# A decode step with attention over a long cache: 210 small transfers of zeros behind every second load

## The chip, the cores and the metric

One core of one Trainium2 chip runs the whole program. The time is that of one launch on the device in microseconds (us). Two runs of the kernel before are shown, 698.48 and 698.58 us, with the median 698.53. A third launch was taken with the hardware profiler; its own time was 698.42 us.

## The reference

One token of each of two sequences goes through attention over a cache of 4096 positions and 32 heads, and then through a small dense block; both are modulated by a condition `c`. Cut to what matters:

```python
mod = (silu(c) @ w_mod).reshape(2, 6, 1, -1)         # w_mod 512 x 3072
sa, ca, ga, sb, cb, gb = (mod[:, i] for i in range(6))
h = layernorm(x) * (1 + ca) + sa                     # x: 2 x 1 x 512
q = (h @ wq).reshape(2, 1, 32, 128).transpose(0, 2, 1, 3)
p = softmax(einsum("bhqd,bhkd->bhqk", q, k_cache) * 128 ** -0.5)
o = einsum("bhqk,bhkd->bhqd", p, v_cache)            # caches: 2 x 32 x 4096 x 128
x = x + ga * (o.transpose(0, 2, 1, 3).reshape(2, 1, 4096) @ wo)
h = layernorm(x) * (1 + cb) + sb
x = x + gb * (mish(h @ w1 + b1) @ w2)                # w1 512 x 1376
```

Everything is float32. The two caches are by far the most of it: 268 of the 297 MB that the launch reads.

## The kernel before

Each weight and each head of the caches is used once, so the kernel streams them all through on-chip memory. `stream` (on the host) packs the pieces into 36 loads. Nearly all of them are one transfer of 128 partitions by 16,384 floats, 64 KB a partition and 8.4 MB in all: the keys of one head (`BIG`, 8192 floats a partition) and other pieces, mostly half heads of the values (`HALF`), that fill it up. The last ones are cut smaller.

`load(n)` takes a buffer called `room` from a pool of three and issues the load's transfers on SP's queue (L141). `used(*keys)` is called when a piece has had its last reader; it issues load n+3 when every piece of load n is used. So SP's queue holds an issue, a wait for a buffer, an issue, and so on, in the order of the loads. Instructions go to each engine in the order in which the program writes them; the framework puts in the waits. It gives each transfer on SP's queue one of eight semaphores in turn (the lanes), and at the end of the program it waits for all of them.

For each of the 32 heads, VectorE multiplies the keys by the query (`products`, L318) and sums over 128 elements (`sums`, L321), each once over 128 x 8192 floats; `row_max` and `soft_max` follow with small instructions. TensorE multiplies the values with the softmax's numerators (`weighted_v`, L359) and does the small projections, ScalarE the exponentials. Load n+1 and n+2 are in flight while head n is worked on.

Behind the last head come the output projection, the second layer norm, the dense block, and the last lines: the result `y`, a buffer of the pool `work` under the tag `sq`, is made by two VectorE instructions (L564, L565) and 32 of its rows of 512 B are stored (L566). GpSimd clears some constants at the start, `cx` first (L160), and SP closes the program at L636.

Of the kernel before, what the change touches and what calls it, by code (L numbers as in the profile page):

```python
# [8 lines left out]
F32 = mybir.dt.float32  # L9
# [4 lines left out]
P = 128  # L14
# [11 lines left out]
OUT_STEP = 4  # L26
AHEAD = (14, 22)
ROW = 2 * BIG


def stream():
# [13 lines left out]
    def size(x):  # L45
        return sum(SIZES[key[0]] for key in x)

    loads = [[([("m01", 0), ("wq", 0), ("wq", 1)], (4 * W,)), ([("k", 0)], (BIG,))]]
    for _ in range(1, HEADS):
        row = []  # L50
        while size(row) < ROW:
            room = ROW - size(row)
            row += order.pop(next(i for i, x in enumerate(order) if size(x) <= room))
        loads.append([(row, (ROW,))])
    last = [("v", h, i) for h in range(HEADS - 4, HEADS) for i in range(2)]
# [14 lines left out]
def kernel(  # L70
# [3 lines left out]
    head: bass.AP,  # L74
    b1c: bass.AP,
    out: bass.AP,
):


# [6 lines left out]
    nc = tc.nc  # L86
# [16 lines left out]
    work = ctx.enter_context(tc.tile_pool(name="work", bufs=2))  # L103
# [12 lines left out]
    def take(t, keys):  # L116
        lo = 0
        for key in keys:
            kind, n = key[:2]
            part = t[:, lo : lo + SIZES[kind]]  # L120
            lo += SIZES[kind]
            if kind == "k":
                k_t[n] = part.rearrange("p (j d) -> p j d", d=DH)
            elif kind == "v":
                v_t[n, key[2]] = part.rearrange("p (c n) -> p c n", n=512)
            elif kind in ("wq", "wo"):
                (wq_t if kind == "wq" else wo_t)[n] = part.rearrange("p (k n) -> p k n", k=G)
            else:
                w_t[kind] = part.rearrange("p (k n) -> p k n", k=NCH if kind == "w2" else G)
# [4 lines left out]
    def load(n):  # L134

        t = kvp.tile([P, ROW], F32, tag="room", name=f"room{n}", bufs=3)
        lo = 0
        for keys, srcs in loads[n]:
            take(t[:, lo:], keys)
            for src in srcs:  # L140
                nc.sync.dma_start(out=t[:, lo : lo + src.shape[-1]], in_=src)  # L141
                lo += src.shape[-1]

    loaded = 0

    def used(*keys):

        nonlocal loaded
        done.update(keys)
        while loaded < len(loads) and (  # L150
            loaded < 3 or all(key in done for keys, _ in loads[loaded - 3] for key in keys)
        ):
            load(loaded)
            loaded += 1
# [16 lines left out]
        out=fold, in_=ident.rearrange("p (g r) -> p r g", g=G), axis=AX.X, op=ALU.add  # L171
# [3 lines left out]
        out=mean_w, in0=fold[:, None, :].to_broadcast([P, G, R]), scalar1=1.0 / D, scalar2=None, op0=ALU.mult  # L175
# [4 lines left out]
        out=half, in_=ident.rearrange("p (b r) -> p r b", b=B), axis=AX.X, op=ALU.add  # L180
# [373 lines left out]
    for n in range(NCH):  # L554
        for t in range(G):
# [4 lines left out]
                start=(n == 0),  # L560
                stop=(n == NCH - 1),
            )
    y = work.tile([P, P], F32, tag="sq", name="y", bufs=1)
    nc.vector.tensor_tensor(out=y, in0=yps[:, :P], in1=mod[5], op=ALU.mult)  # L564
    nc.vector.tensor_tensor(out=y, in0=y, in1=x2, op=ALU.add)  # L565
    nc.sync.dma_start(out=out, in_=y[::OUT_STEP, :])  # L566


def _lay_out(np, a):
# [70 lines left out]
```

## Time and profile before

| | |
|---|---|
| median of two runs | 698.53 us |
| the profiled execution's own time | 698.42 us |
| its span, from first to last instruction | 696.6 us |
| VectorE busy | 587.7 us (84%) |
| TensorE matmuls busy | 283.8 us (41%) |
| ScalarE, GpSimd busy | 44.0 us, 4.2 us |
| read from DRAM | 297.22 MB, 427 GB/s over the span |
| written to DRAM | 0.02 MB |

The DMA part of a profile counts packets. One row of a transfer, contiguous on both sides, is one packet, and the packets of a transfer are dealt over the core's 16 DMA engines. A share of "16 engines" is packet time divided by sixteen times the length of the stretch looked at; a packet is counted whole where it starts, so a short stretch can show over 100%. q1 is SP's queue, q10 ScalarE's, q8 and q14 bring instructions. "SPq" rows are SP's instructions: issuing a transfer, or waiting (EVENT_SEMAPHORE); their durations are minimum, median and maximum in ns.

### The profile page before, as it was taken

How to read it: one execution, taken by the hardware profiler on the slowest of the kernel's cores; microseconds unless marked ns; L12 is line 12 of the kernel's file. 1: busy time of each engine (PE TensorE's matmuls, PEld its weight loads, DVE VectorE, ACT ScalarE, POOL GpSimd, SP SyncE). 2: the span in 40 equal slices, each digit the busy share in tenths (PEclk: the TensorE clock that was granted, in tenths of full speed). 3: DMA queues.
4: the chain of work that ended last, by engine and by line, in shares of the span. 5: the costliest groups of instructions: out<-in, count | busy, mean ns of one | idle time of the engine just before them, and what ended most of it. 6: DMA issues, size and time to landing. Idle time of an engine off the chain costs nothing.

```text
span 696.6 us, 3912 instructions
## 1 busy us (share of the span) xinstructions
PE 283.8 (41%) x1636; PEld 102.4 (15%) x1636; DVE 587.7 (84%) x220; ACT 44.0 (6%) x168; POOL 4.2 (1%) x19
## 2 busy tenths in 40 slices
PE   3403334335245615335232806234333526224686
PEld 1200001001011201102100301011101101001234
DVE  3799899999999999999999999999999999899002
ACT  1000000000000000000000000000000000000010
POOL 2000000000000000000000000000000000000000
PEclk9855666667566665656585756666575657555789
DMA  9999999999999999999999999999999999999996
GB/s 392 452 421 421 426 474 421 419 429 421 467 422 425 429 425 456 429 425 426 433 448 429 426 429 437 440 430 429 433 437 437 429 425 422 452 427 420 423 422 270
DMA packets 6706, 297.49 MB, mean 427 GB/s; under 512 B 888, under 2 KB 928, under 8 KB 1184
## 3 DMA queue, kind: packets, MB, share of 16 engines
q1 hardware_dynamic: 6528, 297.23, 98.9%
q8 instruction: 13, 0.21, 0.1%
q10 hardware_dynamic: 160, 0.01, 0.0%
q14 instruction: 5, 0.04, 0.0%
HBM read 297.22 MB, written 0.02 MB: 427 GB/s over the span
## 4 chain that ended last, share of the span: by engine, by line
DMA 69%; DVE 28%; PE 2%; issue 0%; SPq 0%; ACT 0%; DVEq 0%
DMA room<-in_load 69%; DVE room L318 14%; DVE s L321 14%; PE ov L359 1%; PE qps L291 1%; PE modps L247 1%; PE yps L556 0%; SPq L141 0%; DVE m L334 0%; DVE hcw L280 0%; ACT q L292 0%; PE hps L237 0%; DVE y L564 0%; DVE hq L270 0%; DVE hq L271 0%
## 5 line engine op out<-in xcount | busy, mean ns | idle before, releaser
L318 DVE TENSOR_TENSOR room<-room,q 128x8192 f32<-128x8192 f32 x32 | 278.2, 8692 | 46.8 <-DMA room<-in_load 42.4
L321 DVE TENSOR_REDUCE s<-room 128x64 f32<-128x8192 f32 x32 | 277.9, 8683 | 0.4 <-DVE m L334 0.3
L359 PE MATMUL ov<-room,e 128*32 128x512 f32 x1024 | 176.4, 842 | 80.1 <-ACT e L337 63.9
L330 PE MATMUL mt<-d,same 128*128 128x64 f32 x64 | 18.2, 378 | 195.8 <-DVE d L328 195.8
L359 PEld LDWEIGHTS ov<-room,e 128*32 128x32 f32 x1024 | 39.2, 145 | 188.6 <-issue 133.8
L337 ACT ACTIVATE e<-s,m 64x64 f32<-64x64 f32 x64 | 22.1, 345 | 556.6 <-DVE m L334 555.8
L330 PEld LDWEIGHTS mt<-d,same 128*128 128x128 f32 x64 | 13.1, 254 | 225.8 <-DVE d L328 179.3
L291 PE MATMUL qps<-room,hcw 128*128 128x512 f32 x64 | 43.4, 844 | 4.8 <-DMA room<-in_load 4.0
L345 PE MATMUL l<-l,ones 128*128 128x8 f32 x16 | 4.6, 358 | 75.1 <-ACT e L337 75.1
L382 PE MATMUL otp<-pick,o 128*128 128x8 f32 (+2 forms) x72 | 13.4, 313 | 33.9 <-ACT o L374 32.0
L291 PEld LDWEIGHTS qps<-room,hcw 128*128 128x128 f32 x64 | 16.8, 274 | 26.4 <-issue 20.5
L374 DVE COPY o<-ov 128x256 f32<-128x256 f32 x1 | 0.4, 425 | 22.6 <-ACT o L374 22.6
L382 PEld LDWEIGHTS otp<-pick,o 128*128 128x128 f32 x72 | 12.6, 263 | 42.3 <-ACT o L374 39.4
L345 PEld LDWEIGHTS l<-l,ones 128*128 128x128 f32 x16 | 3.8, 296 | 76.5 <-ACT e L337 76.5
L334 DVE TENSOR_REDUCE m<-mt 128x1 f32<-128x64 f32 x32 | 6.9, 217 | 7.6 <-PE mt L330 7.6
L390 PE MATMUL att<-room,ot 128*32 128x512 f32 x62 | 10.1, 709 | 5.2 <-DMA room<-in_load 4.7
L337 ACT ACTIVATION_READ_ACCUMULATOR e<-s,m 64x1 f32 x64 | 11.8, 185 | 0.0
L328 DVE TENSOR_SCALAR d<-half,m 128x64 f32<-128x64 f32 x32 | 8.1, 254 | 1.1
L247 PE MATMUL modps<-room,ct 128*32 128x128 f32 (+1 forms) x160 | 8.1, 346 | 2.3 <-DMA room<-in_load 2.2
L326 DVE TENSOR_REDUCE m<-s 128x1 f32<-128x64 f32 x32 | 7.0, 217 | 0.9
L374 ACT COPY o<-ov 128x512 f32<-128x512 f32 (+1 forms) x9 | 5.0, 561 | 25.9 <-PE ov L359 25.7
L247 PEld LDWEIGHTS modps<-room,ct 128*32 128x32 f32 x160 | 5.0, 121 | 4.6 <-issue 4.4
(101 smaller groups left out, 60.6 us busy)
## 6 DMA issues: line engine op xcount, KB each, us to landing
room<-in_load SPq DMA_DIRECT2D x4, 4096.0 KB, 25.0
room<-in_load SPq DMA_DIRECT2D x1, 7168.0 KB, 39.1
room<-in_load SPq DMA_DIRECT2D x1, 3072.0 KB, 26.2
room<-in_load SPq DMA_DIRECT2D x3, 1024.0 KB, 28.3
room<-in_load SPq DMA_DIRECT2D x1, 2400.0 KB
room<-in_load SPq DMA_DIRECT2D x1, 2304.0 KB, 20.4
room<-in_load SPq DMA_DIRECT2D x1, 1376.0 KB, 15.8
room<-in_load SPq DMA_DIRECT2D x2, 256.0 KB, 22.8
```

Of the source, the lines that this page charges most:

```text
L247: nc.tensor.matmul(ps[R * g : R * (g + 1)], lhsT=ct[:, k, :], rhs=t[:, k, :].rearrange("p (m n) -> p m n", m=n)[:, :, P * g : P * (g + 1)] ...
L291: nc.tensor.matmul(ps, lhsT=hcw[:, k, :], rhs=wq_t[ch][:, k, :], start=(k == 0), stop=(k == G - 1))
L318: nc.vector.tensor_tensor(out=k_t[h], in0=k_t[h], in1=qv, op=ALU.mult)
L321: nc.vector.tensor_reduce(out=s_t[h], in_=k_t[h], axis=AX.X, op=ALU.add)
L326: nc.vector.tensor_reduce(out=m_t[h][:, 0:1], in_=s_t[h], axis=AX.X, op=ALU.max)
L328: nc.vector.tensor_scalar(out=d, in0=half, scalar1=m_t[h][:, 0:1], scalar2=None, op0=ALU.mult)
L330: nc.tensor.matmul(mps[h], lhsT=same, rhs=d, start=True, stop=True)
L337: nc.scalar.activation(e_t[i][own_b, :, M * i + 4 * b : M * i + 4 * b + 4], s_t[h][own_b].rearrange("p (c m) -> p c m", m=4), AF.Exp, bias ...
L345: nc.tensor.matmul(lps[n], lhsT=ones, rhs=sum_t[n % 2], start=True, stop=True)
L359: nc.tensor.matmul(ov[bank][R * g : R * (g + 1), :], lhsT=e_t[h % HC][:, NB // 2 * part + c, :], rhs=v_t[h, part][:, c, :], start=(first a ...
L382: nc.tensor.matmul(tps[:, x], lhsT=o_t[m], rhs=pick_t[n][:, m, x], start=(m == 0), stop=(m == 3),)
L390: nc.tensor.matmul(att[R * i : R * (i + 1), :], lhsT=ot_t[n % 2][:, i, :], rhs=wo_t[n][:, i, :], start=(n == 0), stop=(n == H // HC - (2 i ...
```

## The change

Behind each odd load from 3 to 29, `load` issues 15 transfers more on SP's queue: the n-th takes n rows of 96 floats (384 B) from `mark`, a buffer of zeros, to its own place in a new DRAM output `marks` that nobody reads. These 210 transfers and the store of the result count on a semaphore of their own, `out_done`, and are taken out of the framework's lanes (`no_tile_sem_insts`). At the end of the program, behind the framework's own closing waits, SP waits until the semaphore stands at 16 x 211 and clears it. `mark` is cleared by GpSimd ahead of its other constants, and `mark` and `y` are buffers of their own instead of pool buffers. No instruction on TensorE, VectorE or ScalarE is added or moved, and the loads keep their order, lanes and waits; the store no longer waits for a lane.

```diff
+MARKED = range(3, 31, 2)
...
             for src in srcs:
                 nc.sync.dma_start(out=t[:, lo : lo + src.shape[-1]], in_=src)
                 lo += src.shape[-1]
+        if n in MARKED:
+            for rows in range(1, 16):
+                m = nc.sync.dma_start(out=marks[MARKED.index(n), rows, :rows], in_=mark[:rows]).then_inc(out_done, 16)
+                tc.no_tile_sem_insts.add(m.ins.name)
 
     loaded = 0
+    nc.gpsimd.memset(mark, 0.0)
...
-    y = work.tile([P, P], F32, tag="sq", name="y", bufs=1)
     nc.vector.tensor_tensor(out=y, in0=yps[:, :P], in1=mod[5], op=ALU.mult)
     nc.vector.tensor_tensor(out=y, in0=y, in1=x2, op=ALU.add)
-    nc.sync.dma_start(out=out, in_=y[::OUT_STEP, :])
+    store = nc.sync.dma_start(out=out, in_=y[::OUT_STEP, :]).then_inc(out_done, 16)
+    tc.no_tile_sem_insts.add(store.ins.name)
...
+    args["out_done"] = nc.alloc_semaphore("out_done")
+    args["mark"] = nc.alloc_sbuf_tensor("mark", [16, 96], F32).ap()
+    args["marks"] = nc.dram_tensor("marks", (len(MARKED), 16, 16, 96), F32, kind="ExternalOutput").ap()
+    args["y"] = nc.alloc_sbuf_tensor("y", [P, P], F32).ap()
     with tile.TileContext(nc) as tc:
         tile_adaln_decode_kernel(tc, **args)
+    nc.sync.wait_ge(args["out_done"], 16 * (1 + 15 * len(MARKED)))
+    nc.sync.sem_clear(args["out_done"])
```

The marked line of the issue is L150 in the changed kernel.

More of the change, by code (lines that the diff above doesn't have):

```diff
@@ L76 @@
     out: bass.AP,
+    out_done,
+    y,
+    mark,
+    marks,
 ):
```

## The prediction

> **What bounds the kernel now.** I read the page first: the span, the slices, the DMA part, the shares of the chain, the two costliest groups.
>
> ```profile
> span 696.6 us, 3912 instructions
> ...
> PE 283.8 (41%) x1636; PEld 102.4 (15%) x1636; DVE 587.7 (84%) x220; ACT 44.0 (6%) x168; POOL 4.2 (1%) x19
> ...
> DMA  9999999999999999999999999999999999999996
> ...
> DMA packets 6706, 297.49 MB, mean 427 GB/s; under 512 B 888, under 2 KB 928, under 8 KB 1184
> ## 3 DMA queue, kind: packets, MB, share of 16 engines
> q1 hardware_dynamic: 6528, 297.23, 98.9%
> ...
> q10 hardware_dynamic: 160, 0.01, 0.0%
> ...
> DMA 69%; DVE 28%; PE 2%; issue 0%; SPq 0%; ACT 0%; DVEq 0%
> ...
> L318 DVE TENSOR_TENSOR room<-room,q 128x8192 f32<-128x8192 f32 x32 | 278.2, 8692 | 46.8 <-DMA room<-in_load 42.4
> L321 DVE TENSOR_REDUCE s<-room 128x64 f32<-128x8192 f32 x32 | 277.9, 8683 | 0.4 <-DVE m L334 0.3
> ```
>
> The 16 DMA engines are busy for 98.9% of their time with SP's queue (q1). VectorE is busy too (84% of the span), but it waits for loads: of its 46.8 us idle ahead of L318, 42.4 end with a load. The chain in order of time shows the rhythm:
>
> ```profile
> 256.49 8.69 DVE room L318
> 265.18 0.14 DVE m L334
> 265.32 8.60 DVE s L321
> 273.97 40.52 DMA room<-in_load
> 314.52 8.69 DVE room L318
> ```
>
> From one L318 to the next on this chain are 314.52 - 256.49 = 58.03 us. There are three buffers, so load n+3 is issued when head n has been summed; the step is three loads, 19.34 us each. VectorE's pair takes 8.69 + 8.69 = 17.4 us of it, so about 2 us lie free. The 40.5 us of DMA are a load that stands behind an earlier one on the engines. A DMA engine that gets more work is therefore late at once, with no cover from VectorE. How full an engine is, a DMA view of 100 to 600 us says:
>
> ```profile
> DMA packets 3708, 216.16 MB, mean 432 GB/s; under 512 B 401, under 2 KB 401, under 8 KB 401
> ...
> q1 hardware_dynamic: 3697, 216.01, 99.9%
> q8 instruction: 8, 0.13, 0.1%
> ```
>
> A full load is 128 packets of 64 KB, eight to an engine, plus one small packet an engine: 401 is 25 loads by 16 and one. On the page, 888 packets under 512 B are the 128 rows of the bias load and 760 = 47 x 16 + 8 others, which fits one semaphore packet for each engine of 45 loads, the bias and the store, and eight for the eight-row load of `cx`. (q10: 128 + 16 + 8 + 8 = 160.) So a transfer of eight rows used eight engines. One 64 KB packet lasts 0.999 x 16 x 500 us / 3296 = 2.42 us, and 0.1% of 8000 us, 8 us with a rounding of 4 either way, is left over at 400 load ends: 10 to 30 ns for each, semaphore packet and next load following.
>
> **The added transfers on the engines.** MARKED has 14 loads (3, 5, ... 29), with 15 transfers of 1 to 15 rows behind each. If a transfer of n rows uses n engines and always begins at the same one, that engine carries 15 row packets and 15 semaphore packets a group, 14 x 15 = 210 pairs in all, and the last engine almost none; if the beginning moves round, each has 14 x 120 / 16 = 105 pairs. No row shows which engines are used. I take 210, the dearer end; 105 stays as the lower bound.
>
> The nearest thing to such a pair is the output store: 32 rows of 512 B, two to an engine, on idle engines. The DMA view from 695.25 to 695.46 us, then from 695.44 to 695.46 us (one semaphore packet), then its issue and landing:
>
> ```profile
> DMA packets 48, 0.02 MB, mean 78 GB/s; under 512 B 16, under 2 KB 48, under 8 KB 48
> ...
> q1 hardware_dynamic: 48, 0.02, 30.3%
> ```
>
> ```profile
> q1 hardware_dynamic: 1, 0.00, 2.8%
> ```
>
> ```profile
> out<-y SPq DMA_DIRECT2D x1, 16.0 KB, 1.7
> ...
> 694.06 0.55 SPq L566 DMA_DIRECT2D out<-y  x1
> ```
>
> The semaphore packet is 0.028 x 16 x 20 ns = 9 ns. All 48 are 0.303 x 16 x 210 = 1018 ns; less 16 x 9, a row of 512 B is 27 ns. A row of 384 B lies on the line between 4 B at 9 and 512 B at 27: 23 ns. A pair is 32 ns of packets; with the idle 10 to 30 ns at a load's end it is 42 to 62. I take 42, the low end, as rows of a store followed each other in the 210 ns window: 210 x 42 = 8.8 us, between 6.7 (no gap) and 13.0 (30 ns).
>
> From that goes the slack of the loaded engine. Engines do not run level: of load 31's semaphore packets, seven stand in 602.40 to 603.40 us, eight in 604.20 to 605.10, the last in 605.60 to 605.80:
>
> ```profile
> DMA packets 15, 0.52 MB, mean 524 GB/s; under 512 B 7, under 2 KB 7, under 8 KB 7
> ```
>
> ```profile
> DMA packets 19, 0.72 MB, mean 801 GB/s; under 512 B 8, under 2 KB 8, under 8 KB 8
> ```
>
> ```profile
> DMA packets 2, 0.07 MB, mean 328 GB/s; under 512 B 1, under 2 KB 1, under 8 KB 1
> ```
>
> An engine is ahead of the last one by 0 to 3.3 us, in the mean by (7 x 2.8 + 8 x 1.05) / 16 = 1.75 us. A load is complete with its slowest engine, so 8.8 - 1.75 = 7.0 us arrive at the end; behind load 29 nothing is marked, and the last loads only pass the delay on.
>
> The Trainium skill ("DMA: Bandwidth & Descriptors", Why a DMA increments its semaphore by 16 and not by 1) says that a transfer on SP's queue takes the lowest-numbered k engines, k the largest number up to 16 that divides the slowest dimensions of both sides. By it the 15-row transfer uses 15 engines and the same engine is hit each time: my 210, and the count of eight for `cx` agrees; with a moving start the sum would be 698.4 + 105 x 42 ns = 702.8 us.
>
> **The issues on SP.** SP's rows of the load line:
>
> ```profile
> L141 SPq DMA_DIRECT2D room<-in_load x45: 327/328/530, 0.7 to 670.0; - x45
> L141 SPq EVENT_SEMAPHORE  x36: 17/17522/17887, 12.9 to 662.0; - x36
> ...
> DMA to landing us min/median/max: 12.2/40.5/59.2
> ```
>
> Fifteen issues at 0.33 us, or at the store's 0.55, are 4.9 to 8.2 us. Behind them waits only the next load's issue, and SP sits 17.5 us (median) in its wait for that load's buffer: hidden, with 9 us left. Were that cover gone, the next load would still have about 19 us of queued work ahead of it on the engines. Some 210 more instructions are fetched too: q8 brought 0.13 MB / 8 = 16 KB at a time, 0.6 us of one engine at 64 KB in 2.42; a fetch or two more, mostly on other engines, is counted at nothing.
>
> **Start and end.** The clear of `mark` stands ahead of that of `cx` on GpSimd, and the first mark waits for it.
>
> ```profile
> 0.00:13.00 13.00, 1.71 (x6) 1.51 (x7) 5.13 (x19) 1.93 (x4) 3.79 (x18) 1.00 0.89 364
> ...
> SPq L636 <- DMA out<-y: 0.9, 1, 0.9
> ```
>
> GpSimd's 18 clears take 3.8 us of the first 13 (the fifth busy column), while the first load takes 12.2 to land (the least of the landings above); one more costs nothing, and the first group comes only behind load 3. At the end SP waited 0.9 us for the store at L636; that wait now stands behind the framework's closing steps, with a clear of the semaphore after it. Between 1 us gained and 1 lost, I take 0. The own buffer for `y` adds no wait.
>
> **Sum.** The profiled execution's own time is 698.42 us (span 696.6 and 1.8 around it), 0.1 below the median of 698.53. 698.4 + 7.0 = 705.4; I say 705.
>
> **Rivals.** (1) Slower: a pair holds its engine until the write has landed, so pairs cannot overlap. The store's last packet ends near 695.46 and its landing is at 694.06 + 1.7 = 695.76: 0.3 us of landing a pair at least, 1.7 at most. 210 x 0.3 - 1.75 = +61, 760 us; at 1.7 us +355, 1054. It decides from 210 pairs of 76 ns, where 2% is passed. Against it speak the 10 to 30 ns at a load's end; for it, that a load has one semaphore packet per engine in 19 us, whose stall a buffer may hide, and a group has 15 in a row. Chance 0.12.
>
> The Trainium skill (same page, Anatomy of one DMA, written for GpSimd's path) calls most of a small transfer's fixed 2 us a wait for the write's receipt, ahead of the semaphore. Our store's 1.7 us agrees in size; whether the engine stands idle meanwhile no run here shows.
>
> (2) A row of 384 B costs double, as a read and a write: 2 x 27 + 9 + 10 = 73 ns a pair, 210 x 73 = 15.3, less 1.75: 712 us; up to 722 if it is threefold and gaps are 30 ns (210 x 120). Nothing in the trace is a store under 512 B. Chance 0.13, half of it over 2%.
>
> The Trainium skill (same page, Specifications) says that under 512 B the engine does a read-modify-write; no run here shows its price.
>
> (3) Two loads and 15 marks are 17 transfers in flight on one queue; if it holds fewer, SP is stopped in mid-group until the marked load drains, and engines run dry.
>
> ```profile
> 667.40 2.98 SPq L141 DMA_DIRECT2D room<-in_load  x6
> ```
>
> Six issues in 2.98 us went through unhindered, and no issue of 45 took over 0.53; 17 at once are not seen. With some six marks left (6 x 0.35), the next load's issue and its 1.2 us to the first packet (695.25 - 694.06), 3.6 us of dry engines a group: 14 x 3.6 = 50, 748 us. Chance 0.10.
>
> (4) It does less than it says: pairs spread over all engines (702.8), or the loaded engine has the full 3.3 us of slack and pairs cost 25 ns (+2, 700.4). Chance 0.10.
>
> **How the numbers follow.** The forecast, 700 to 712, has 0.54; the rivals 0.12, 0.13, 0.10 and 0.10; 0.01 stays for a gain over 2%, which 16 full engines exclude but for a reason I don't see. 2% (14 us) is about what a measurement here tells from no change. Within it: 0.54 + 0.10 + 0.07 = 0.71; slower 0.06 + 0.12 + 0.10 = 0.28. The range 699 to 725 takes in the forecast, (4) and (2), and leaves (1) and (3) out.
>
> **What would show it.** Right: q1 has 14 x 240 = 3360 packets more; in a marked load's end the engines' semaphore packets spread by 0.6 us a group, one engine falling behind the rest until it ends each load; the L318 step grows from 58.0 to about 59 us. Wrong: a step longer by several us with idle gaps on one engine (1) or on all (3), an L150 issue of many us on SP (3), or marked groups that move no engine against another (4).

## The result and the profile after

The changed kernel takes 721.51 us (721.29 and 721.74), the kernel before 698.53: a ratio of 1.0327, 95% interval 1.0311 to 1.0344, 23.0 us more where 6.5 were forecast. The profiled execution took 721.74 us. Its page, with the span, the packets, SP's DMA queue, the chain's shares and VectorE's two large groups:

```profile
span 720.0 us, 4123 instructions
...
DMA packets 10067, 298.15 MB, mean 414 GB/s; under 512 B 4248, under 2 KB 4288, under 8 KB 4544
...
q1 hardware_dynamic: 9888, 297.88, 97.7%
...
DMA 70%; DVE 27%; PE 2%; issue 0%; SPq 0%; ACT 0%; DVEq 0%
...
L328 DVE TENSOR_TENSOR room<-room,q 128x8192 f32<-128x8192 f32 x32 | 278.1, 8692 | 71.1 <-DMA room<-in_load 65.2
L331 DVE TENSOR_REDUCE s<-room 128x64 f32<-128x8192 f32 x32 | 277.9, 8683 | 0.4 <-DVE m L344 0.3
```

q1 has 9888 - 6528 = 3360 packets more, as forecast. VectorE's work is the same to 0.1 us; its idle time ahead of L328 (L318 before) grew by 24.3 us, 22.8 of them waits for loads. So the time came in through late loads. The chain in order of time (start, length, what) shows by how much for each group:

```profile
142.74 8.69 DVE room L328
151.53 8.70 DVE s L331
160.29 42.45 DMA room<-in_load
202.76 8.69 DVE room L328
211.55 8.70 DVE s L331
220.30 44.36 DMA room<-in_load
264.76 8.69 DVE room L328
```

Steps of 60.02 and 62.00 us alternate, as one marked load or two fall into three. Six loads with three groups take 122.0 us, against 2 x 58.03 before: 2.0 us a group, three times the 0.6 that the forecast's working gives (15 x 42 ns). 14 x 2.0 less the spread of 3.3 us that the engines had from before would be 24.7.

Where are the 2.0 us? Two DMA views of one engine's group: the 16 semaphore packets and 15 rows in 202.25 to 202.63 us, then the one 64 KB packet that starts behind them. The third is a 64 KB packet of the kernel before, in a stretch of the same length (10 ns, so the share is its length over 160 ns).

```profile
DMA packets 31, 0.01 MB, mean 15 GB/s; under 512 B 31, under 2 KB 31, under 8 KB 31
...
q1 hardware_dynamic: 31, 0.01, 7.8%
```

```profile
q1 hardware_dynamic: 1, 0.07, 2542.5%
```

```profile
q1 hardware_dynamic: 1, 0.07, 1511.9%
```

The small packets are as quick as forecast: 31 of them in 0.38 us, 25 ns a pair. But the packet behind them lasts 25.425 x 160 = 4.07 us, where 15.119 x 160 = 2.42 is usual. 0.38 + 1.65 = 2.03 us: the group's whole price, and most of it is paid by the next load. So something behind the packets' records backs up, by inference; the experiments ask what.

SP's rows, the marks' and the loads':

```profile
L150 SPq DMA_DIRECT2D marks<-mark x210: 251/296/410, 42.7 to 572.1; - x105
```

```profile
L146 SPq EVENT_SEMAPHORE  x36: 17/15722/19452, 13.0 to 686.6; - x36
```

No issue is held up (0.41 us at most), and SP still waits 15.7 us (median) ahead of a load. At the end, from the store's issue at 718.24 us to the span's end are 1.76 us; before, 694.06 to 696.6, 2.54:

```profile
718.24 0.55 SPq L575 DMA_DIRECT2D out<-y  x1
```

### The profile page after: what moved, and what is told of

It is laid out like the page before. It is cut to its first block, busy times and chain, and to the rows that moved or that the text cites. A ratio compares the mean times of both kernels' runs of the same rounds, so it can differ in the third digit from the quotient of the medians.

```text
span 720.0 us, 4123 instructions
## 1 busy us (share of the span) xinstructions
PE 286.4 (40%) x1636; PEld 105.6 (15%) x1636; DVE 587.6 (82%) x220; ACT 44.0 (6%) x168; POOL 4.3 (1%) x20
## 3 DMA queue, kind: packets, MB, share of 16 engines
q1 hardware_dynamic: 9888, 297.88, 97.7%
## 4 chain that ended last, share of the span: by engine, by line
DMA 70%; DVE 27%; PE 2%; issue 0%; SPq 0%; ACT 0%; DVEq 0%
DMA room<-in_load 70%; DVE room L328 13%; DVE s L331 13%; PE ov L369 1%; PE qps L301 1%; PE modps L257 1%; SPq L146 0%; PE yps L566 0%; DVE m L344 0%; DVE hcw L290 0%; PE hps L247 0%; ACT q L302 0%; DVE y L573 0%; DVE hq L281 0%; DVE hq L280 0%
## 5 line engine op out<-in xcount | busy, mean ns | idle before, releaser
L328 DVE TENSOR_TENSOR room<-room,q 128x8192 f32<-128x8192 f32 x32 | 278.1, 8692 | 71.1 <-DMA room<-in_load 65.2
L302 ACT ACTIVATE q<-qps 128x512 f32<-128x512 f32 x8 | 4.8, 598 | 14.6 <-PE qps L301 14.5
```

Of the source, the lines that this page charges most:

```text
L328: nc.vector.tensor_tensor(out=k_t[h], in0=k_t[h], in1=qv, op=ALU.mult)
```

## The experiments

Three theories stood for the long packet. Landing: each transfer's semaphore packet holds its engine's write side until what it stands for has landed, and what is read behind it backs up. Short rows: writing a row of 384 B is dear. Late reads: small packets fill the engine's look-ahead, so that the next 64 KB are read late. Medians are beside a kernel before of 698.55 to 698.59 us; what is written to `marks` is read by nobody. The count that the last wait expects and the shape of `marks` follow each edit; such lines are not shown (`...`).

**Rows of 512 B**, taken from `ones` (made a buffer of its own, as in the other kernels that read it).

```diff
-                m = nc.sync.dma_start(out=marks[MARKED.index(n), rows, :rows], in_=mark[:rows]).then_inc(out_done, 16)
+                m = nc.sync.dma_start(out=marks[MARKED.index(n), rows, :rows], in_=ones[:rows]).then_inc(out_done, 16)
...
-    args["marks"] = nc.dram_tensor("marks", (len(MARKED), 16, 16, 96), F32, kind="ExternalOutput").ap()
+    args["marks"] = nc.dram_tensor("marks", (len(MARKED), 16, 16, 128), F32, kind="ExternalOutput").ap()
```

> The same 210 transfers, with rows of 512 B in place of 384 B. In the changed kernel the 64 KB packet behind 15 pairs (row and semaphore) on one engine took 4.06 us in place of 2.42. Short rows (writing a row under 512 B is what holds the engine): that packet is back at 2.4 us and the time at 702 to 705 us. Landing (each transfer's semaphore packet holds the engine's write side until its row has landed) and late reads (the small packets take the place of the look-ahead, so that the next 64 KB are read late): the packet stays near 4.06 us and the time at 721 to 722 us.

721.67 us, 1.0329 (1.0299 to 1.0359). A 64 KB packet behind a group, in a stretch of 10 ns:

```profile
q1 hardware_dynamic: 1, 0.07, 2477.5%
```

24.775 x 160 = 3.96 us. Short rows are out.

**One transfer with 15 rows for each engine**, so 15 rows and one semaphore packet.

```diff
-            for rows in range(1, 16):
-                m = nc.sync.dma_start(out=marks[MARKED.index(n), rows, :rows], in_=mark[:rows]).then_inc(out_done, 16)
-                tc.no_tile_sem_insts.add(m.ins.name)
+            m = nc.sync.dma_start(
+                out=marks[MARKED.index(n), :, :, :96], in_=ones[:16, None, :96].to_broadcast([16, 15, 96])
+            ).then_inc(out_done, 16)
+            tc.no_tile_sem_insts.add(m.ins.name)
...
```

> One transfer behind each marked load, with 15 rows of 384 B for each of the 16 engines: 15 row packets but one semaphore packet an engine. Short rows: every engine is held as the fullest one was, about 14 x 1.9 us with no slack, 724 to 727 us. Landing: one landing a group instead of 15, 14 x 15 x 19 ns = 4 us, 702 to 704 us, and the next 64 KB packet at 2.4 us. Late reads: 16 packets stand where 30 stood, as with seven or eight pairs, whose next packet was 0.4 to 0.8 us long: 708 to 714 us.

701.34 us, 1.0041 (1.0025 to 1.0057). The 64 KB packet behind 15 rows (a stretch of 6 ns, so the share is over 96 ns):

```profile
q1 hardware_dynamic: 1, 0.07, 2518.8%
```

25.188 x 96 = 2.42 us, as without marks. As many rows as on the fullest engine before, here on all 16, cost 2.8 us instead of 23. The 14 transfers fewer, each with its semaphore, are the difference; late reads had 708 to 714.

**Fifteen pairs on all 16 engines.**

```diff
-                m = nc.sync.dma_start(out=marks[MARKED.index(n), rows, :rows], in_=mark[:rows]).then_inc(out_done, 16)
+                m = nc.sync.dma_start(out=marks[MARKED.index(n), rows], in_=mark).then_inc(out_done, 16)
```

> Fifteen transfers of 16 rows each, so that all 16 engines carry 15 pairs a group instead of the first alone. All three theories, if an engine is held by its own pairs alone: 14 x 2.0 us with no slack to use up, 725 to 728 us, and the next 64 KB packet near 4.06 us on every engine. If the engines share what holds them (one place where semaphores or rows are written): clearly longer than 730 us.

729.00 us, 1.0434 (1.0404 to 1.0464): twice the rows and semaphores cost 7.5 us more than the changed kernel, a little over the range. The trace shows why: the engines do not hold equally long. These are 64 KB packets behind the last group, in stretches of 10 ns, on an early engine (606.99 us) and on a late one (615.01 us):

```profile
q1 hardware_dynamic: 1, 0.07, 2323.8%
```

```profile
q1 hardware_dynamic: 1, 0.07, 2820.6%
```

23.238 x 160 = 3.72 us and 28.206 x 160 = 4.51 us. The 16 long packets of the first group start within 0.7 us (80.23 to 80.88), those of the last within 8.9 (606.77 to 615.63), and the late ones are the longest: the same engines are slow each time. The slowest lose 0.38 + 2.09 = 2.5 us a group. 14 x 2.5 = 35 us, less the 3.3 us of slack seen before and the 1.4 us that the end gains (the last run below), is 30, and 30.4 were measured.

**Rows to on-chip memory.** The rows are 64 B and go to `spot`, an on-chip buffer, and the store is back in its lane.

```diff
+                lo = rows * (rows - 1) // 2
-                m = nc.sync.dma_start(out=marks[MARKED.index(n), rows, :rows], in_=mark[:rows]).then_inc(out_done, 16)
+                m = nc.sync.dma_start(out=spot[lo : lo + rows, MARKED.index(n)], in_=ones[:rows, :16]).then_inc(out_done, 16)
...
```

> The same 15 transfers of 1 to 15 rows, from ones, to on-chip memory in place of DRAM, with rows of 64 B for want of room, and the result's store back in its lane as before the change. Short rows (in DRAM): the cost goes, 701 to 704 us. Landing: a load's semaphore landed 0.4 to 0.5 us after its packet, the store's 0.3, so no less than in the changed kernel, 718 to 730 us. Late reads: the packets are as many, 719 to 721 us.

723.69 us, 1.0358 (1.0328 to 1.0388). DRAM as the target isn't what costs.

**29 rows, one semaphore**: the same edit as for 15 rows, with 29.

```diff
-                out=marks[MARKED.index(n), :, :, :96], in_=ones[:16, None, :96].to_broadcast([16, 15, 96])
+                out=marks[MARKED.index(n), :, :, :96], in_=ones[:16, None, :96].to_broadcast([16, 29, 96])
...
```

> One transfer behind each marked load with 29 rows of 384 B and one semaphore packet for every engine: 30 small packets an engine, as many as the fullest engine of the changed kernel had, but one semaphore in place of 15. Landing: the rows alone, 14 x 29 x 19 ns = 7.7 us at most, 704 to 706.5 us, and the next 64 KB packet at 2.4 us. Late reads (the number of small packets decides): 721 to 727 us.

705.72 us, 1.0103 (1.0074 to 1.0132). 30 small packets an engine, as behind each marked load of the changed kernel, at a third of its price: late reads is out. The rows alone cost 7.2 us (8.6 with the end's gain of 1.4, the last run below), near the 14 x 29 x 19 ns = 7.7 of their packets.

**Thirty pairs.**

```diff
-            for rows in range(1, 16):
-                m = nc.sync.dma_start(out=marks[MARKED.index(n), rows, :rows], in_=mark[:rows]).then_inc(out_done, 16)
-                tc.no_tile_sem_insts.add(m.ins.name)
+            for copy in range(2):
+                for rows in range(1, 16):
+                    to = marks[MARKED.index(n), copy, rows, :rows]
+                    m = nc.sync.dma_start(out=to, in_=mark[:rows]).then_inc(out_done, 16)
+                    tc.no_tile_sem_insts.add(m.ins.name)
...
```

> The 15 transfers twice in a row behind each marked load, 30 pairs on the fullest engine. In the changed kernel 15 pairs held it 15 x 25 + 1640 = 2010 ns: 134 ns a pair, or 190 for each past the first five. Landing: it goes on growing, 4.0 to 4.9 us a group, 14 x that less some 3 us of slack, 750 to 765 us, and the next 64 KB packet 5.5 to 7 us long. Late reads: one latency at most, so 14 x 0.37 us more than the changed kernel, 727 us, and the packet stays near 4.1 us.

760.17 us, 1.0883 (1.0851 to 1.0914). It goes on growing. A 64 KB packet behind a group, again in 10 ns, lasts 32.344 x 160 = 5.18 us, less than the 5.5 to 7 expected:

```profile
q1 hardware_dynamic: 1, 0.07, 3234.4%
```

But a second thing is in this run. SP's rows of the marks and of the loads:

```profile
L152 SPq DMA_DIRECT2D marks<-mark x420: 251/296/7199, 41.0 to 620.1; - x140
```

```profile
L146 SPq DMA_DIRECT2D room<-in_load x45: 328/425/7115, 0.7 to 734.2; - x45
```

Issues are now held for up to 7.2 us: 30 marks and two loads are more than the queue takes without stopping SP. How much of the 61.6 us that adds isn't separated, so the 0.184 us a pair that the next expectations use, (61.6 - 23.0) / 210, is not clean.

**Five transfers a group.**

```diff
-            for rows in range(1, 16):
+            for rows in range(11, 16):
...
```

> Five transfers a group (11 to 15 rows), five pairs on the fullest engines. Behind five pairs the next 64 KB packet was hardly longer in the changed kernel (median 0.06 us). Landing with a buffer that takes up the first pairs, and late reads too: 699 to 701 us. Landing in which each semaphore costs its full 134 ns: 14 x 5 x 0.134 less some 2 us, 705 to 708 us.

701.35 us, 1.0031 (1.0017 to 1.0045), with runs from 699.75 to 701.65: just over the range of the theory with a buffer and far under that of the full 134 ns. Most of five pairs' hold is taken up by something.

**All on one engine.**

```diff
-                m = nc.sync.dma_start(out=marks[MARKED.index(n), rows, :rows], in_=mark[:rows]).then_inc(out_done, 16)
+                m = nc.sync.dma_start(out=marks[MARKED.index(n), rows, :1], in_=mark[:1]).then_inc(out_done, 16)
```

> Fifteen transfers of one row each, so that 210 pairs lie on the first engine alone and no other engine has any (1680 row packets in the changed kernel, 210 here). If an engine is held by its own semaphores: 720 to 722 us, as in the changed kernel. If the semaphores of all engines queue at one place: well under, 703 to 712 us. If one-row transfers move from engine to engine: 14 pairs each, 699 to 702 us.

723.23 us, 1.0354 (1.0324 to 1.0384). An eighth of the rows and semaphores gives the whole price; that it is 1.2 us over the range stays open. One-row transfers all go to one engine, and what that engine carries itself decides; the semaphores don't queue at a place that the engines share.

The trace also has the times at which `out_done` was counted up. In the changed kernel, once the fullest engine alone was still at work on a group (us):

```
610.863 611.045 611.228 611.410 611.593 611.773 611.953
```

0.18 us apart, while the packets' records come every 25 ns. With the rows written to on-chip memory they are as far apart, at the end of that run's last group:

```
612.478 612.660 612.840 613.020
```

15 x 0.18 = 2.7 us a group; 2.03 show in the packets' records. The other 0.7 us are hidden, by inference in what the engine has read and not yet written.

**Seven transfers a group, on ScalarE's queue and on SP's.**

```diff
-            for rows in range(1, 16):
-                m = nc.sync.dma_start(out=marks[MARKED.index(n), rows, :rows], in_=mark[:rows]).then_inc(out_done, 16)
+            for rows in range(9, 16):
+                m = nc.scalar.dma_start(out=marks[MARKED.index(n), rows, :rows], in_=mark[:rows]).then_inc(out_done, 16)
...
```

> Seven transfers a group (9 to 15 rows), issued on ScalarE's queue instead of SP's. At the start of every run the small packets of ScalarE's queue alternate with SP's loads, so each semaphore would stand behind a 64 KB packet and its hold be hidden: 698.3 to 700 us, and no 64 KB packet longer than 2.5 us behind them. If a semaphore holds its engine wherever it stands: 14 x 7 x 0.18 = 18 us and no buffer between, 712 to 717 us. If ScalarE's instructions are held by the issues and VectorE waits for them: over 702 us.

```diff
-            for rows in range(1, 16):
+            for rows in range(9, 16):
...
```

> Seven transfers a group (9 to 15 rows) on SP's queue, beside the seven on ScalarE's. With 0.184 us a pair, 0.95 us hidden a group and 2.3 us of slack once: 14 x (7 x 0.184 - 0.95) - 2.3 = 2.4, 700 to 703 us. If hidden only by the slack: 14 x 7 x 0.184 - 2.3 = 15.7, 714 us.

On ScalarE's queue 698.94 us, 1.0003 (0.9994 to 1.0013). Against the end alone (697.23 us, the last run below) that is 1.7 us, no more than the 98 x 25 ns = 2.5 us of its pairs' packets. On SP's 706.33, 1.0111 (1.0096 to 1.0126), which is 9.1 us by the same measure. The DMA view of the first, 46 to 56 us:

```profile
DMA packets 120, 4.60 MB, mean 460 GB/s; under 512 B 50, under 2 KB 50, under 8 KB 50
...
q1 hardware_dynamic: 70, 4.59, 105.8%
q10 hardware_dynamic: 50, 0.01, 0.5%
```

Its 50 small packets of q10 are spread among 70 large ones, with 2.42 us of load between two on an engine, and 13 of its 3968 64 KB packets last over 2.5 us, where the kernel before has 12. So each hold seems to be over before the next semaphore comes. On SP's queue seven cost more than expected (700 to 703). Nine engines carry seven pairs there, and again they differ: the 126 packets behind their groups last 2.76 to 3.09 us. One behind the last group, on a late engine (593.05 us):

```profile
q1 hardware_dynamic: 1, 0.07, 1913.8%
```

19.138 x 160 = 3.06 us, 0.64 more than usual. With 7 x 25 ns that is 0.8 us a group, 11.4 in all. Less the end's 1.4 and up to 3.3 of slack, 6.7 to 10 are left, and 7.7 were measured. The 0.95 us taken as hidden in a group was too much.

**Seven and eight behind each load** instead of 15 behind every second.

```diff
-MARKED = range(3, 31, 2)
+MARKED = range(3, 31)
...
-            for rows in range(1, 16):
-                m = nc.sync.dma_start(out=marks[MARKED.index(n), rows, :rows], in_=mark[:rows]).then_inc(out_done, 16)
+            for rows in range(1, 16)[n % 2::2]:
+                m = nc.sync.dma_start(out=marks[(n - 3) // 2, rows, :rows], in_=mark[:rows]).then_inc(out_done, 16)
...
```

> The same 210 transfers, the even row counts behind odd loads and the odd ones behind even loads: 7 and 8 pairs a time on the fullest engine in place of 15 behind every second. From 15 to 30 pairs the time grew by 0.184 us a pair, and 15 pairs cost 15.6 us in all less than 14 x 15 x 0.184: taken as 0.95 us hidden in each group and 2.3 of slack once, 38.6 - 28 x 0.95 - 2.3 = 9.7, 706 to 711 us. If the hold is the same for each semaphore however they stand together: 721 us.

710.40 us, 1.0170 (1.0155 to 1.0185): the same 210 transfers at half the price, so something is hidden anew in each group.

**The end alone**: no marked load.

```diff
-MARKED = range(3, 31, 2)
+MARKED = ()
...
```

> No marked loads: only the store's own semaphore, waited for behind the framework's closing steps, the clear of mark, and y and mark as buffers of their own. Counted at nothing: 698.0 to 699.0 us. If the end carries part of the added 23 us: over 700 us.

697.23 us, 0.9981 (0.9971 to 0.9990): 1.4 us faster than before, and the one version here that beats both kernels. From the store's issue (693.73 us) to the end of the span (695.5 us) are 1.77 us, as in the changed kernel, 0.8 less than before:

```profile
span 695.5 us, 3913 instructions
```

```profile
693.73 0.55 SPq L575 DMA_DIRECT2D out<-y  x1
```

The store's landing now runs beside the framework's closing steps. The rest of the 1.4 us is not located. Every other version here but the one with on-chip rows has the same end, so by this measure its marks cost 1.4 us more than its difference from the kernel before: 24.3 us in the changed kernel.

## Why the prediction was wrong

**The bound: right.** SP's queue on full engines sets the step, and VectorE gives no cover: the loads came later by what the group took.

**The count: right.** 210 pairs lie on the fullest engine. One-row transfers put all of theirs on one engine at the same price (723.23 us).

**The price of a pair: wrong, and this is the step that failed.** "A pair is 32 ns of packets; with the idle 10 to 30 ns at a load's end it is 42 to 62." The packets are 25 ns a pair, even less. But the packets' records do not show when a transfer has landed: the semaphores are counted 0.18 us apart when they stand close together, and the engine is held meanwhile, which shows in the next load's packet. The profile of before could not show that: 64 KB packets stood between two semaphores of an engine, and the ScalarE run shows that with so much in between a hold costs no more than the packets. The 10 to 30 ns at 400 load ends were thus no upper bound for 15 in a row. Worked back in the prediction's own terms, (23.0 + 1.75) / 210 = 118 ns a pair are on the path, outside the 42 to 62.

**The slack: too small, but a minor term.** 14 x 2.03 = 28.4 us of hold on the fullest engine arrive as 23.0. The end's gain is 1.4 of the difference and about 4 us are slack, where 1.75 were taken off and 3.3 were named as the most.

**Rival (1) named the hold**, with the reason that a load's single hold may be hidden and 15 in a row not, and priced it at 0.3 us or more from the store's landing, 760 us. The runs show 0.18 us, of which 0.7 us a group are hidden: 2.0 us a group. The price could have been bounded from both sides, with the packets' pitch as the lower end and the landing as the upper; the forecast took the lower one as if it were near. In the Trainium skill ("DMA: Bandwidth & Descriptors", Anatomy of one DMA, written for GpSimd's path) the write's receipt ahead of the semaphore is the larger part of a small transfer's fixed cost. The runs agree that a cost hangs on the transfer with its semaphore and not on the rows, at 0.18 us each. What the engine waits for stays open: the receipt, the semaphore's own write and the transfer as such are told apart by no run, since each transfer brings one semaphore to an engine. On-chip rows have the same 0.18 us, so it is not DRAM as the target.

**Rival (2)**, short rows: wrong. 512 B cost the same, and 29 rows of 384 B under one semaphore 7.2 us. The read-modify-write below 512 B that the Trainium skill states ("DMA: Bandwidth & Descriptors", Specifications) left no mark in this time. The measured 721.5 us lies inside the range of 699 to 725 only because that was widened for this rival, whose upper price was 722: this is luck, as the forecast itself, 700 to 712, was passed.

**Rival (3)**, a full queue: not at 17 transfers (issues of 0.41 us at most; with all 16 engines carrying 15 pairs one of 210 took 1.53), but there at 32 (7.2 us).

**Issues, start and end.** SP's issues were hidden as reckoned. The end, counted between 1 us gained and 1 lost, gains 1.4, a little more than the bound.

## What to carry to other kernels

Behind a stream that fills the DMA engines, count the transfers on the fullest engine, each with its semaphore, and not the bytes: 15 in a row held it 2 us, while 29 rows under one semaphore on every engine cost 0.6. Put many rows into one transfer, or issue small transfers on a queue where large packets of another stand between them: seven a group cost 9.1 us on the loads' queue and 1.7 on ScalarE's, both against the end alone. And packet records that follow each other closely don't show that an engine is free: look at the length of the next large packet.

## What the runs showed that was not expected

A transfer's delay can stand in the record of the packet behind it: 4.07 us in place of 2.42 for the same 64 KB. And the engines differ: 15 pairs a group on each of 16 engines cost 30.4 us and on one engine 24.7, more than 3.3 us of slack between engines accounts for. The slowest engines lose 2.5 us a group where the first loses 2.0; the miss with seven on SP's queue has the same cause. Why some engines are slower no run shows.
